# Batch 0's linear attention by token slot on 64x64 tiles, with the carried state added in PSUM, in a gated linear attention and channel mixer kernel on one Trainium2 core

## The chip, the cores and the metric

The kernel runs on one core of one Trainium2 chip. The metric is the device time of one execution in microseconds (us): three runs of the kernel before took 166.55, 166.55 and 166.72, median 166.55. The engines of a core are called as in the profile: PE (TensorE; PEld is its weight load), DVE (VectorE), ACT (ScalarE), POOL (GpSimd) and SP (SyncE, which here only issues transfers). Transfers are issued by SP and by ACT, each on a queue of its own.

## What is computed

Four batches, eight heads, 768 tokens, 48 channels per head. First a gated linear attention with a carried 48x48 state per head, then a mixer over tokens and one over channels, all on the 384 channels of the eight heads side by side:

```python
for t in range(S):
    state = alpha[:, :, t, :, None] * state + np.einsum('bhd,bhe->bhde', k[:, :, t], v[:, :, t])
    y[:, :, t] = np.einsum('bhd,bhde->bhe', q[:, :, t], state)
...
xt = x.transpose(0, 2, 1)
h = np.maximum(xt @ w_tok1, 0.0) @ w_tok2
u = x + h.transpose(0, 2, 1)
h2 = np.maximum(u @ w_ch1, 0.0) @ w_ch2
return (u + h2).astype(np.float32)
```

w_tok1 is 768x256, w_tok2 256x768, w_ch1 384x1536, w_ch2 1536x384; inputs and output are float32.

## The kernel before

**Chunks.** The attention is done in chunks of 256 tokens, three per batch, numbered n = 0 to 11 over all batches (batch 0 is n = 0, 1, 2). A chunk lies with two neighbouring tokens per partition: token 2p + s of the chunk is in partition p, in token slot s (0 or 1). Partitions 0 to 63 are its half 0 (128 tokens), 64 to 127 its half 1. Each chunk loads alpha, k, q and v, 384 KB each (`ld_at`, `ld_kt`, `ld_qt`, `ld_vt`; L534).

**Decay.** The recurrence is made parallel by cumulative products of alpha: logarithms on ACT (`ln`), cumulative sums by a matmul with a triangular matrix (`cumw` for batch 0, `cum` for the others), exponentials on ACT (`E`, `IE`, and `Et` for the decay of a whole half). k is multiplied by IE (`kk`, L642), q by E (`qq`). Batch 0 (`WIDE`) does this for both slots apart; the others first multiply the alphas of the two slots (`P`, L578) and adjust k and q (`k0a`, `q0r`).

**Within a chunk.** k and q are transposed on PE (`trk`, `trq`) and copied out of PSUM (`evk`, `evq`); from n = 6 on transfers do it (`dk`, `dq`, `pq`). `G` (gmm) makes the products of k and q for one half, 128x128 per head, as 16 matmuls on 64x64 tiles; `mask` (L700) copies them with a causal mask. `y` (ymm) multiplies them with v, contracting over the 128 tokens of a half in one matmul per head; `i` (inter) adds q times the state carried into that half; `x` copies the result as the mixer's input, 128 tokens by 384.

**The halves.** To contract over 128 tokens of one half, its two slots must fill 128 partitions, while they lie in 64 partitions side by side. So half tiles are copied to the other partitions: of v by `vs0`, `vs1` (vswap), of k by `ka`, `kb`, `kc` (kturn; `kc` overwrites k in place, after `trk`). `K` (kfull) then makes both halves' sums of k times v, four matmuls each. The state after a half is (K + state before) times the decay: `sa` adds (L750, DVE), `sm` multiplies (L753, DVE or POOL); `s` (L747) is the multiplication alone where there is no state before.

**Mixer.** Per batch: `t1` (L787, 12 matmuls in two groups), relu `ht`, `t2` (L792, six results, each reads both pieces of w_tok2), `u` = x + t2 (L796), `up` transposes u on PE (L803) and `ut` copies it, `c1` (L811: 12 chunks of 128 of the 1536 columns, two halves of the tokens each, three matmuls of 384), relu `rt`, `c2` (L816: four groups of three matmuls for each of six token blocks), `o` adds u (L820), `st` stores. From batch 2 on a transfer transposes u (`ux`).

**Weights.** They are loaded in pieces of 384 KB (`ldw_`) and cast to bf16 (`cw_`): wt1 and wt2 in two pieces each, wc1 in six (piece 3h + c is the half h of the columns, 128 of the 384 rows), wc2 in six.

**Order.** Nothing is scheduled when the kernel is built: `ORDER` lists every operation with its engine as the last letter (t PE, s ACT, v DVE, g POOL, y SP), and each engine runs its own in that order. `BUFS` gives the buffer of each tile in turn. Waits follow from the data and the buffers; an operation that overwrites a buffer waits for its readers. All raw loads share the buffers of class `in`, of which there are 19. An operation marked `port` (the copies and products that both DVE and POOL can do) also waits for the last marked one on the other of these two engines (`shared`). A transfer signals on one of eight semaphores, and waits for the transfer that last used its semaphore. Fillers (`f1_`, `f3_`) are matmuls of zeros, 512 wide, that keep PE busy before an operation.

## Time and profile before

| | us |
|---|---|
| median of three runs | 166.55 |
| span of the profiled execution | 165.0 |
| busy: PE, DVE, ACT, POOL | 156.2, 121.2, 96.2, 68.7 |
| busy in the first 30 us: PE, DVE, ACT, POOL | 24.4, 21.6, 23.1, 14.9 |
| matmuls of zeros (x38) | 12.7 |
| c1 and c2 matmuls (x588) | 106.0 |

The profiled execution's own time is the span and what lies around it; 1.55 us separate the span from the median of the runs. The granted clock reads full in every slice. PE waited longest for a first result of DVE (1.2 us in two waits), for the memset of the zeros (1.1) and for two copies on ACT (1.0 and 0.9).

Line numbers with L are those of the kernel before. Matmuls go through a helper, so L593 stands for many of them, and L684 and L685 for the copies on ACT and on DVE or POOL. Times in the timeline are the start in us from the start of the span, and the duration.

### The profile page before, as it was taken

The page shows a single profiled execution, that of the slowest core. Times are in us where ns is not written, and L with a number is a line of the kernel's source. Part 1 is how long each engine was busy: PE and PEld are TensorE (multiplying, and loading weights), DVE is VectorE, ACT ScalarE, POOL GpSimd, SP SyncE. Part 2 cuts the span into 40 slices and gives each one's busy share as a digit, 9 for nine tenths or more (in the row PEclk, how much of TensorE's full clock was granted, in tenths as well). Part 3 has the DMA queues.
Part 4 walks back from the last instruction along what each step waited for, and adds up shares of the span by engine and source line. Part 5 has one row for each costly group of instructions (what it writes and reads, how often), then busy time and mean ns, then how long its engine had stood idle before and what let it go on. Part 6 is the DMA issues. An engine that isn't in the chain of part 4 may idle for free.

```text
span 165.0 us, 4235 instructions
## 1 busy us (share of the span) xinstructions
PE 156.2 (95%) x1683; PEld 99.2 (60%) x1683; DVE 121.2 (73%) x210; ACT 96.2 (58%) x186; POOL 68.7 (42%) x84
## 2 busy tenths in 40 slices
PE   7969769999999999999999999999999999999992
PEld 2435446666666766576666666666666656656662
DVE  4098989989898898798878999989492455524422
ACT  3599987998877837939887746913614001514110
POOL 4025659497217475792388528973300000000000
PEclk9999999999999999999999999999999999999999
DMA  4999999999999999999989996898001136200213
GB/s 121 324 325 325 337 347 316 365 327 352 371 335 347 326 315 226 307 252 264 136 198 255 211 250 120 219 181 183 0 4 48 49 75 157 105 0 0 99 72 119
DMA packets 74531, 34.48 MB, mean 209 GB/s; under 512 B 67984, under 2 KB 73488, under 8 KB 74512
## 3 DMA queue, kind: packets, MB, share of 16 engines
q1 hardware_dynamic: 50576, 23.30, 55.2%
q10 hardware_dynamic: 23936, 10.91, 24.3%
q8 instruction: 13, 0.21, 0.5%
q14 instruction: 6, 0.05, 0.1%
HBM read 25.17 MB, written 4.72 MB: 181 GB/s over the span
## 4 chain that ended last, share of the span: by engine, by line
PE 83%; DMA 4%; SPq 3%; POOL 2%; issue 2%; ACT 2%; DVE 1%; POOLq 0%; DVEq 0%
PE ps L816 29%; PE ps L811 29%; PE ps L593 14%; PE ps L792 5%; DMA in<-in_v_dram 4%; PE ps L787 4%; SPq L534 3%; PE ps L654 1%; PE ps L803 1%; POOL pkk L642 1%; DVE gtm L700 1%; POOL vb L685 1%; ACT x L684 1%; POOL ss L753 1%; ACT E L626 0%
## 5 line engine op out<-in xcount | busy, mean ns | idle before, releaser
L816 PE MATMUL ps<-wc,rt 128*128 128x384 bf16 (+1 forms) x300 | 54.7, 320 | 0.0
L811 PE MATMUL ps<-ut,wc 128*128 128x384 bf16 x288 | 51.3, 326 | 0.0
L782 ACT ACTIVATE rt<-ps 128x384 bf16<-128x384 f32 x54 | 24.4, 490 | 35.4 <-PE ps L811 34.7
L811 PEld LDWEIGHTS <-wc 128*128 128x128 bf16 x288 | 27.1, 98 | 16.7
L816 PEld LDWEIGHTS <-rt 128*128 128x128 bf16 x300 | 27.5, 98 | 15.9
L700 DVE TENSOR_TENSOR gtm<-ps,mk 128x1024 bf16<-128x1024 f32 x24 | 28.7, 1219 | 4.8 <-PE ps L593 3.4
L784 DVE TENSOR_SCALAR rt<-ps 128x384 bf16<-128x384 f32 x42 | 21.7, 551 | 9.2 <-PE ps L811 9.2
L820 DVE TENSOR_TENSOR o<-ps,u 128x384 f32<-128x384 f32 (+1 forms) x25 | 13.1, 537 | 10.0 <-PE ps L816 9.1
L685 POOL CAST vb<-in 64x384 bf16<-64x384 f32 (+1 forms) x18 | 10.9, 608 | 15.2 <-DVE pkk L642 8.9
L593 PE MATMUL ps<-zs 128*128 128x512 bf16 x38 | 12.7, 452 | 2.9 <-DVE zs L496 1.1
L684 ACT CAST x<-ps 128x384 bf16<-128x384 f32 x17 | 7.8, 477 | 10.7 <-PE ps L593 10.5
L796 DVE TENSOR_TENSOR u<-ps,x 128x384 bf16<-128x384 f32 x24 | 11.8, 550 | 3.0 <-PE ps L792 3.0
L642 DVE TENSOR_TENSOR pkq<-in,E 128x768 bf16<-128x768 f32 x8 | 7.6, 954 | 5.4 <-ACT E L626 5.2
L787 PE MATMUL ps<-x,wt 128*128 128x384 bf16 x48 | 11.1, 325 | 0.5 <-DVE gtm L700 0.4
L684 ACT CAST vb<-in 64x384 bf16<-64x384 f32 (+1 forms) x18 | 11.1, 618 | 0.7 <-DMA in<-in_v_dram 0.2
L642 POOL TENSOR_TENSOR pkk<-in,IE 128x768 bf16<-128x768 f32 x5 | 9.1, 1816 | 4.9 <-DVE pkk L685 3.2
L753 POOL TENSOR_TENSOR ss<-tmp,E 128x384 bf16<-128x384 f32 x11 | 9.2, 833 | 3.2 <-DVE tmp L750 2.9
L750 DVE TENSOR_TENSOR tmp<-ps,ss 128x384 f32<-128x384 f32 x16 | 8.8, 552 | 1.0 <-PE ps L593 0.5
L792 PE MATMUL ps<-ht,wt 128*128 128x384 bf16 x48 | 9.5, 326 | 0.0
L593 PEld LDWEIGHTS <-gtm 128*128 128x128 bf16 x192 | 7.4, 96 | 2.7 <-DVE gtm L700 0.9
L593 PEld LDWEIGHTS <-tpk 48*64 48x64 bf16 x384 | 6.1, 106 | 4.9 <-issue 4.3
L593 PE MATMUL ps<-vb,gtm 128*128 128x48 bf16 x192 | 8.6, 183 | 0.4 <-DVE gtm L700 0.4
(91 smaller groups left out, 216.6 us busy)
## 6 DMA issues: line engine op xcount, KB each, us to landing
in<-in_moe_w_ch_dram SPq DMA_DIRECT2D x10, 384.0 KB, 6.2
in<-in_alpha_dram SPq DMA_DIRECT2D x9, 384.0 KB, 6.8
out_dram<-o SPq DMA_DIRECT2D x16, 192.0 KB, 2.5
in<-in_q_dram SPq DMA_DIRECT2D x7, 384.0 KB, 6.3
in<-in_v_dram ACTq DMA_DIRECT2D x7, 384.0 KB, 6.0
in<-in_k_dram ACTq DMA_DIRECT2D x6, 384.0 KB, 5.7
in<-in_k_dram SPq DMA_DIRECT2D x6, 384.0 KB, 6.2
in<-in_v_dram SPq DMA_DIRECT2D x5, 384.0 KB, 7.2
```

The source lines that it names most:

```text
L593: return self.pe.matmul(out, lhsT=lhsT, rhs=rhs, start=start, stop=stop, skip_group_check=True)
L642: self.shared(self.eng[e].tensor_tensor(self.t(dst)[:, :, :, 0:D], self.t(src).rearrange("p h s d -> p s h d"), bass.AP(tensor=f.tensor, o ...
L684: return self.act.copy(d, s)
L685: return self.shared(self.eng[e].tensor_copy(d, s))
L700: self.nc.vector.tensor_tensor(self.t(gtm)[:, hf, :, :], self.pair(gp).rearrange("p a (j t) -> p (a j) t", t=128), bass.AP(tensor=m.tensor ...
L782: self.act.activation(d, s, AF.Relu)
L784: self.nc.vector.tensor_scalar_max(d, s, 0.0)
L787: self.pe.matmul(self.bank(bank)[:, 0:HD], lhsT=self.wt1[:, kc, m * 128 : m * 128 + 128], rhs=self.t(x), start=(kc == 0), stop=(kc == NS - 1))
L792: self.pe.matmul(self.bank(bank)[:, 0:HD], lhsT=self.wt2[:, kc, i * 128 : i * 128 + 128], rhs=self.t(hts[kc]), start=(kc == 0), stop=(kc = ...
L811: self.pe.matmul(self.bank(bank)[:, 0:HD], lhsT=self.wc1[:, kc, mc * 128 : mc * 128 + 128], rhs=self.t(ut)[:, 3 * half : 3 * half + 3, kc, ...
L816: self.pe.matmul(self.bank(bank)[:, 0 : cz - ca], lhsT=self.t(rts[mc][0])[:, i * 128 : i * 128 + 128], rhs=self.wc2[:, mc, ca:cz], start=( ...
L820: self.nc.vector.tensor_tensor(self.t(o)[:, ca:cz], self.bank(bank)[:, 0 : cz - ca], self.t(u)[:, i % 3, ca:cz], ALU.add)
```

## The change

**Batch 0 by token slot.** For n = 0, 1, 2 the two slots stay where they lie. `gslot` computes for one slot of k (instead of one half) the products with q: output partitions 0 to 63 hold half 0's tokens of that slot, 64 to 127 half 1's. `maskslot` uses a mask for each slot (`mkw`, built by eight small copies at the start), still 128x1024 per instruction. `khalf` sums k times v on 64x64 tiles, per half, head pair and slot, 16 matmuls of 48 columns; `kadd` adds the state before in PSUM by one matmul with the identity; `s` then multiplies by the decay on DVE. `yslot` makes both halves of y in 32 matmuls that contract over 64 partitions. The copies `vs`, `ka`, `kb`, `kc` and the additions `sa` of batch 0 are gone. Chunks from n = 3 on do as before.

**Weight pieces.** Pieces 0 to 2 of wc1 are now 256 columns with all 384 rows each, so that chunks 0 to 5 of `c1` wait for one piece alone; pieces 3 to 5 are as before. The matmuls of zeros read a buffer of the relus instead of a tile of their own.

**Order.** `ORDER` and `BUFS` are new throughout: 954 operations are 923; of 22 fillers (38 matmuls) 5 are left (18 matmuls, eight of them before `cumw0`); of the 64 loads ACT issues 30, where it issued 24 (11 of the first 24, where it was 4 of the first 25); the loads use buffers 0 to 11 of class `in`, where they used all 19.

```diff
+        if wide:
+            for hf in range(nst):
+                kp, s_, sp = V("one"), V("ss"), states[-1]
+                KO = O(f"K{hf}_", {"PE": (160.0, 350.0)}, 9.5 + hf, writes=[kp], reads=[pkk, vb],
+                       preds=[kk, vc] + fill(f"K{hf}_", kp),
+                       emit=lambda e, hf=hf, kp=kp, sp=sp: g.khalf(kp, pkk, vb, hf, sp is not None), mode="G")
+                if sp is not None:
+                    KO = O(f"A{hf}_", pe([384]), 9.6 + hf, writes=[kp], reads=[sp[0]], preds=[KO, sp[1]],
+                           emit=lambda e, kp=kp, s0=sp[0]: g.kadd(kp, s0))
+                so = O(f"s{hf}_", dve(384), 10 + hf, writes=[s_], reads=[kp, E], preds=[KO, et],
+                       emit=lambda e, s_=s_, kp=kp, hf=hf, sp=sp: g.sfirst(s_, kp, E, hf, wide, sp is not None))
+                states.append((s_, so))
+        else:
...
+        if wide:
+            yo = O("y", {"PE": (640.0, 830.0)}, 14, writes=yps, reads=[gtm, vb], preds=masks + [vc] + helds[0] + helds[1],
+                   emit=lambda e, st=states[:2]: g.yslot(yps, gtm, vb, [not q for q in st]), mode="Y")
...
-                         reads=[ut], preds=(uts[0:2 + half] if b in UP else [uts[half]]) + [wl[("wc1", mc // 6 * 3 + p)] for p in range(3)],
+                         reads=[ut], preds=(uts[0:2 + half] if b in UP else [uts[half]]) + [wl[("wc1", p)] for p in ([mc // 2] if mc < 6 else (3, 4, 5))],
...
+        for h in (slice(0, 64), slice(64, 128)):
+            for sl in range(2):
+                w = self.mkw[h, sl].rearrange("p (t s) -> p s t", s=2)
+                dv.tensor_copy(w[:, 1], self.u2[h, h])
+                dv.tensor_copy(w[:, 0], (self.us if sl else self.u2)[h, h])
...
+    def gslot(self, gp, tpk, tpq, sl):
+        tk, tq = self.t(tpk), self.t(tpq)
+        for j in range(4):
+            for hf in range(2):
+                for r in range(2):
+                    pr = slice(r * 64, r * 64 + D)
+                    self.mm(self.bank(gp, r)[hf * 64 : hf * 64 + 64, j * 128 : j * 128 + 128],
+                            tk[pr, (sl * 4 + j) * 128 + hf * 64 : (sl * 4 + j) * 128 + hf * 64 + 64],
+                            tq[pr, j * 256 + hf * 128 : j * 256 + hf * 128 + 128], True, True)
...
+    def khalf(self, kp, pkk, vb, hf, spread):
+        kk, vv = self.t(pkk), self.t(vb)
+        ph, w = slice(hf * 64, hf * 64 + 64), 2 * D if spread else D
+        for j in range(4):
+            for sl in range(2):
+                for r in range(2):
+                    c = w * j + (D * r if spread else 0)
+                    self.mm(self.bank(kp)[r * 64 : r * 64 + 64, c : c + D], kk[ph, sl, 2 * j + r, :],
+                            vv[ph, sl, 2 * j + r, :], j == 0 and sl == 0, not spread and sl == 1)
+
+    def kadd(self, kp, s0):
+        self.mm(self.bank(kp)[:, 0:HD], self.idn, self.t(s0), False, True)
+
+    def yslot(self, yps, gtm, vb, first):
+        gg, vv = self.t(gtm), self.t(vb)
+        for h in range(H):
+            for sl in range(2):
+                for hf in range(2):
+                    ph = slice(hf * 64, hf * 64 + 64)
+                    self.mm(self.bank(yps[hf])[:, h * D : h * D + D], gg[ph, sl, 4 * (h % 2) + h // 2, :],
+                            vv[ph, sl, h, :], first[hf] and h == 0 and sl == 0, h == H - 1 and sl == 1)
```

The orders begin so (before, then after); a load is `ld_` or `ldw_` with its engine as the last letter:

```
ld_at1s ld_at0y ld_qt0y ld_vt0y ld_kt0s ld_at2y f1_cumw0t ln0s f3_cumw0t f1_trk1t f1_cumw1t f1_trk0t f3_cumw1t
f1_trq0t f3_trq0t ln1s ld_qt1y f1_trq1t cumw0t cumw1t E0s ld_at3y f3_trk1t IE0s Et0s qq0v vb0s ld_kt1y kk0v trq0t E1s
f3_cumw2t vs1_0g ld_vt1y evq0v trk0t ka0s vs0_0g f1_cumw2t evk0s ld_kt3y qq1v kb0s IE1s f1_G00t G0_0t P3g ld_qt2y
...
```

```
ld_at0s ln0s f8_cumw0t cumw0t ld_at1y ln1s ld_kt0y IE0s cumw1t Et1s kk0g f6_trk0t f1_trk0t trk0t E0s E1s ld_qt0y qq0v
f1_trq0t trq0t ld_at2y evk0v ld_vt0y vb0g ln2s cumw2t ld_kt1s Et0s K0_0t IE1s ld_qt1y kk1v qq1g evq0s E2s ld_qt2s qq2g
K1_0t G0_0t s0_0v Et2s ld_vt1y G1_0t trk1t mask1_0v IE2s ld_at3s evk1s f2_trq1t trq1t vb1s ib0t A1_0t ld_kt2y mask0_0v
P3v ld_kt3y ld_vt2y s1_0v y0t trq2t K0_1t x0_0v kk2v ld_vt3s evq1s G0_1t x1_0s lnP3s A0_1t s0_1v ldw_wt10s evq2s ln13s
ld_qt3s cum3t k0a3g IE3s G1_1t mask1_1v kk3g vb3g mask0_1v ldw_wt11s ldw_wt21s trk2t K1_1t A1_1t ldw_wt20y evk2s E3s
r13s G1_2t mask1_2v G0_2t ldw_wc14y vb2s kb3g ib1t ia1t y1t ld_at4s ka3s trk3t ldw_wc13y K0_2t s1_1v A0_2t cw_wt10s
t1_0_1_0t x0_1s t1_0_0_0t mask0_2v vs1_3s t1_0_0_1t ldw_wc15s t1_0_0_2t vs0_3g cw_wt11s ia2t kc3g K3t ld_kt4y s0_2v
ib2t y2t x1_1s ldw_wc12y t1_0_1_1t t1_0_1_2t q0r3g qq3g t1_0_0_3t x0_2s evk3v t1_0_1_3t t1_0_1_4t cw_wt20g s0_3v x1_2v
...
```

## The prediction

> **What bounds the kernel now.** I read the granted clock and the 40 slices first, then the chain of waits in order of time, the table of stretches, the landings of the loads, and the timeline of the first 37 us on each engine. In the slices (the page's second part) PE and DMA say most:
>
> ```profile
> PE   7969769999999999999999999999999999999992
> DVE  4098989989898898798878999989492455524422
> PEclk9999999999999999999999999999999999999999
> DMA  4999999999999999999989996898001136200213
> ```
>
> From the seventh slice on PE is busy 90% or more, to the end; the clock is granted in full; DMA is full for the first half, and DVE has little to spare until slice 29. The chain gives the seam exactly (start, duration, what):
>
> ```profile
> 9.15 1.15 SPq L534
> ...
> 10.34 1.15 SPq L534
> ...
> 14.06 7.23 DMA in<-in_v_dram
> ...
> 31.39 0.86 PE ps L787 x4
> ...
> 32.99 2.06 PE ps L792 x12
> ...
> 37.51 2.48 PE ps L811 x15
> ...
> 156.81 5.16 PE ps L816 x42
> 161.97 0.03 issue
> 162.02 0.04 issue
> 162.06 0.36 DVE o L820
> ```
>
> Up to 31.4 us loads and vector work set the pace: SP's queue lets one 384 KB load through every 1.15 to 1.26 us. From 31.39 to 162.0 the chain is PE without a gap over 0.04 us, then one result and its store, 3.0 us. So the end is the moment from which PE has no more gaps, plus the PE work then left. The change alters batch 0's attention, nearly all before that moment. I therefore compare the first channel-mixing matmul (L811), 37.51 in the row, and what PE has done by then. Token mixing's second matmuls (L792) start at 32.99.
>
> The landings, in us after the issue, from stretches at 9.2, 14.5 and 17.1 us:
>
> ```profile
> in<-in_k_dram SPq DMA_DIRECT2D x1, 384.0 KB, 4.8
> ...
> in<-in_k_dram ACTq DMA_DIRECT2D x1, 384.0 KB, 5.9
> ...
> in<-in_moe_w_tok_dram ACTq DMA_DIRECT2D x1, 384.0 KB, 5.7
> ```
>
> SP's load waits behind its own queue; ACT's two had nearly none of their own, and yet took longer. The trace's packets of that k load on ACT's queue run only from 17.26 to 19.81: 2.7 us after the issue, then 2.55 us beside SP's, against 1.21 for a load that runs alone. An ACT load costs 5.8 us while SP's queue is full; a second behind it comes 2.5 us later.
>
> **The change part by part.**
>
> **Vector work taken out.** Thirteen half copies (vs six, ka and kb two each, kc three; 0.50 on POOL, 0.51 on ACT, L684 and L685) make 6.6 us, four additions (L750, 0.56) 2.2 us; four multiplications stay, now on DVE from PSUM (L747, 0.55). 8.8 us over three engines is 2.9 us at the best, if nothing else ends last. Setup gains eight small mask copies on DVE; the same engine waits 5.2 us for the first exponential (before 8.52), which hides them (0.2 us each by L519's row, 1.6 us if bare).
>
> **PE.** K takes 80 matmuls where 20 were, y 96 where 48 were, 4 additions by the identity come in: 112 more net, of small size. No row shows them; the nearest is G's (L593, 64x64 tiles), 0.42 us for 16 alone, 0.285 in the chain: 2.0 to 2.9 us. PE's useful work in the first 30 us is some 24.4 (the stretches) less 12.7 of filler: 18 us of cover, so I take zero; at the end of a chain, y's 32 cost at most 0.4 more than before. Fillers go from 38 to 18.
>
> **The clock at the start.** The fillers' weight loads come 0.427 us apart until the row at 5.72, and 0.2 after: full speed came after 4.7 us of unbroken work. Now eight fillers end 3.4 us after the first, and PE stands until the first logarithm ends. That starts at 5.6 instead of 5.0, its load now being ACT's (landing rows 4.8 against 4.2), so the first cumulative sum starts at 6.5 (6.62 before). I take half speed for both sums: 1.7 us each for 0.88 (L593 rows at 6.62 to 7.50). Bounds: 0 and 1.6 us. The Trainium skill ("TensorE: Matmul & The Clock Gate", Part 1) says that a busy free-running window of about 3.4 us releases the clock; by it the sums would be slow here unless a window fell just on the fillers, the same 1.6 us; the 4.7 us of the rows above agree with a window that began after the first filler.
>
> **Loads.** Of the first 24 loads 11 are now ACT's (4 of 25 before), and they rotate over 12 buffers instead of 19, so more wait for a reader. Step by step, ACT's load at 5.3 us (between 4.8 and 5.8) where its queue is empty:
> - k of n=1 is issued behind ln2, after the second sum's Et1: 10.2, landing 15.5. Before: issued 9.15, landed 13.95, kk1 at 14.54. Now kk1 starts 15.6 and ends 16.5.
> - Behind kk1 on DVE stand s0_0 and both masks of n=0, to 19.4 (0.5 and twice 1.17). alpha of n=3 goes into kk1's buffer: issued 16.6, landing 21.9. P3, on POOL at 12.94 before, is now on DVE and waits for it, 2.5 us, with s1_0, x0_0, kk2 and three masks queued behind.
> - From P3 to x1_2 stand seven 384-wide operations (0.48 apart), kk2 (0.86), four masks (1.17), evk3 (0.65): 9.6. x1_2 runs 31.5 to 32.05. Before, the last x (ACT, L684) ended at 31.72.
> - wt10 is issued behind lnP3, 22.4, landing 28; on the same queue follow qt3, wt11, wt21 at 1.2 to 2.5 each: wt21 lands between 31.6 and 33 (27.5 before). Its cast (0.83) stands on ACT ahead of ht_0_0: 32.4 to 33.8. On POOL, each operation waiting for its marked neighbour on DVE, k0a3, kk3 (1.82), vb3, three halves, q0r3, qq3 (1.82) put the cast of wt20 at 32.05.
> So three chains meet at t2: last three t1 (0.5), drain 0.2, ht 0.55 after x1_2 give 33.4; wt21 33 to 34.3; wt20 32.1. I take 33.4, +0.4 on 32.99. From there to L811 the row of before needs 4.52, 0.27 of it a sum of n=5 that now comes later: 33.4 + 4.25 = 37.65. The third of the three pieces that c1's first chunk needs, wc15, is last but one on ACT's queue (behind at4): landing 36.4 to 37.4, cast 0.82: 37.2 to 38.2, no later in the middle. That the other half of wc1 comes in pieces that serve two chunks alone gives nothing here, as chunk 11 is first and needs three whole pieces. Its shorter runs (1024 B) cost nothing by wt1's row, 5.7.
>
> **Later stages.** From L811 on, work is the same; the 0.27 us sum is still to do. Counted on PE's order with these rows, three places now have 0.8 to 1.0 us of PE work between a c1 and the c2 that reads its relu (1.2 was the least), and the chain needs 0.2 + 0.5 + 0.07. DVE's share falls by about 10 us (work goes to POOL), so I charge 0.1 each: 0.3; bounds 0 and 1.5.
>
> Sum: 0.14 + 0.27 + 0.3 = +0.7 us on the profiled execution: span 165.0 becomes 165.7. The median of the runs is 1.55 above that span; with it 167.3.
>
> **The rivals.**
>
> *Loads land as with SP (4.8, no sharing).* Then kk1 starts 14.9, alpha lands 20.9, x1_2 ends 31.0, wt21 lands by 30.4; with a clock that is released a further 1.1 comes off. t2 at 31.3 to 32.3, L811 at 35.6 to 36.6, the removed 2.9 us showing in part: -1.9 to -0.9, less 0.27 and some of the 0.3 given back: 164.9 to 166.0. For it: before, SP's queue alone moved as many bytes. Against: the two ACT rows above, and 2.5 us of DVE standing for P3. 0.36.
>
> *The ACT queue starves channel mixing* (the other side). wt21 and wc15 take 2.5 us each because kt4, wc12, at5 and qt4 run on SP beside them. wt21 at 33, wc15 at 38.2 or a load later, 39.4, cast 0.8: L811 at 39 to 40, 1.5 to 2.5 later: 168.3 to 169.5. It decides from wc15 landing after 36.8. For it: DMA is full up to slice 18. Against: SP itself waits for casts in between. 0.15.
>
> *Later weights come late.* Twelve buffers let loads run less far ahead: wc22 and wc23 are issued by ACT at about 45 and 48 and land 5.8 later, and second mixing wants them at 53.7 and 57. Missing by one load costs 1.2, by two 2.4 us: 168.5 to 169.7. For it: DMA shows no free slice before the 20th. Against: the order asks for no load early that it does not need. 0.09.
>
> *64x64 does not pay.* If the four quarters do not overlap, each matmul still costs no more than the 0.02 to 0.026 us of G's rows; the 18 us of cover takes it. It gives the forecast's time.
>
> **How the numbers follow.** The forecast has 0.40, and by its own bounds (clock released, wt21 at 31.6 or at 33) 166.1 to 167.9. About 0.2% (0.33 us) is what a measurement here can tell from no change: 0.05 of the forecast's chance and 0.02 of the first rival's lie within it, 0.02 of the forecast's below. Faster: 0.34 + 0.02 = 0.36; same 0.07; slower: 0.33 + 0.15 + 0.09 = 0.57. The range takes the first rival's good end with 0.3 for a quicker alpha load, and the later-weights rival nearly whole: 164.6 to 169.8.
>
> **What would show it.** L792 starting near 33.4 and L811 near 37.6, with ACT's wt21 cast just ahead. P3 (L578) on DVE with an idle of 2 to 3 us put down to the alpha load. kk1 (L642, DVE) at 15 to 16. First sums with 0.32 us matmuls. PE full from L811 on, but for a few tenths. I am wrong if ACT's loads land in under 5 us, if L811 starts before 36.5, or if PE has over 1 us of gaps behind it.

## The result, and the profile after

The changed kernel takes 182.8 us (median of 4 runs, 181.0 to 183.4) against 166.55 us (166.46 to 166.72) for the kernel before: a ratio of 1.093, 95% interval 1.086 to 1.100. It is slower, as forecast, but by 16.3 us where 0.7 was forecast and 169.8 was the end of the range. The profiled execution has a span of 179.3 us (165.0 before). Executions more than 1.5% above the fastest of their kernel are left out of the ratios and times below (one of s6 took 863 us, which nothing here explains); the profiles of a9 and s5 are of such executions, and so these two have no start and rest.

The first view is again the 40 slices of the span, one digit for the busy tenths of each:

```profile
PE   7595679998899989999896999989889999999972
DVE  6035369777598966759787977979593551563412
PEclk9998765799999999999999999999999999999997
DMA  5999989997999976999999986796700133212042
```

Before, PE was at 9 from the seventh slice to the last but one. Now it is at 5 to 7 in four of the second to sixth slice, and behind them it falls to 8 in turns and once to 6. DMA, which was full from the second to the 20th slice, has holes from the sixth on. And the granted clock, which was full, is below that from the fourth to the eighth slice, with 5 in the seventh as the lowest.

Two numbers split the loss. The first matmul of channel mixing (L863, L811 before) starts at 41.67 instead of 37.34 us: 4.3 us are lost ahead of it. From there to the end of the span it takes 137.6 instead of 127.7 us: 10.0 us are lost behind it. (Second token mixing starts at 37.44 instead of 32.90.) I call these two the start and the rest below; the rest is the span less the start.

Ahead of the seam, DVE's timeline shows what was late first (start, duration, engine, line, operation; in brackets the idle time before it and what ended it):

```profile
16.95 2.36 DVE L740 TENSOR_TENSOR gtm<-ps,mkw 128x1024 bf16<-128x1024 f32 x2 [0.63 <-PE ps L617]
24.19 0.56 DVE L602 TENSOR_TENSOR in<-in 128x384 f32<-128x384 f32 x1 [4.88 <-DMA in<-in_alpha_dram]
24.66 0.55 DVE L799 TENSOR_TENSOR ss<-ps,E 128x384 bf16<-128x384 f32 x1
```

The product P3 waits 4.9 us for alpha of group 3. DVE has nothing else it may do, since s1_0, x0_0, kk2 and three masks stand behind it. That load was issued on ScalarE's queue at 15.88, and the landings of the stretch from 13 to 17 us give its time:

```profile
in<-in_moe_w_ch_dram SPq DMA_DIRECT2D x2, 384.0 KB, 7.1
...
in<-in_alpha_dram ACTq DMA_DIRECT2D x1, 384.0 KB, 8.2
```

The second row is that load: 8.2 us, and not 5.3 as I took it. What stands behind it is in ScalarE's timeline (ACT is its work, ACTq the loads that it issues):

```profile
21.16 0.48 ACT L708 CAST x<-ps 128x384 bf16<-128x384 f32 x1
24.78 0.52 ACT L608 ACTIVATE la<-in 128x384 bf16<-128x384 f32 x1 [3.14 <-DVE in L602]
24.86 0.38 ACTq L568 DMA_DIRECT2D in<-in_moe_w_tok_dram  x1
...
25.34 1.22 ACTq L552 DMA_DIRECT2D in<-in_q_dram  x1
...
26.71 0.49 ACTq L568 DMA_DIRECT2D in<-in_moe_w_tok_dram  x1
...
27.23 0.50 ACTq L570 DMA_DIRECT2D in<-in_moe_w_tok_dram  x1
```

These rows are one chain. lnP3 (L608) waits for P3, and P3 for alpha. The load of wt10 is *behind lnP3 in the same queue*, so it is issued at 24.86, and q of group 3, wt11 and wt21 follow it. A late load holds up work, and that work holds up the next loads: from 20 to 34 us the DMA engines move 283 GB/s, against 341 in the kernel before (mean of the stretches 20 to 26 and 26 to 34, by length).

Behind the seam there is no single place. The waits of PE from 41 us to the end (who waited for whom, sum in us, times, longest):

```profile
PE ps L863 <- ACT rt L834: 1.6, 1, 1.6
PE ps L868 <- DVE o L872: 1.4, 1, 1.4
PE ps L863 <- DMA ut<-u: 1.0, 1, 1.0
PE ps L617 <- DVE ss L805: 1.0, 1, 1.0
PE ps L617 <- DVE tmp L802: 0.9, 1, 0.9
PE ps L868 <- ACT wc L708: 0.6, 1, 0.6
PE ps L617 <- ACT rt L834: 0.5, 1, 0.5
PE ps L863 <- DVE rt L836: 0.5, 1, 0.5
```

The same view of the kernel before is empty: not one wait long enough to be listed. The eight waits make 7.5 of the 10.0 us; the other 2.5 are in no single row. The first line is at 45 us, and ScalarE's timeline gives its reason: two loads of the first channel weight take ScalarE's sequencer 1.99 us to issue, a third load 0.50, and behind them stand two logarithms and the relu that PE needs, which comes at 45.09.

```profile
41.53 1.99 ACTq L573 DMA_DIRECT2D in<-in_moe_w_ch_dram  x2
43.55 0.50 ACTq L552 DMA_DIRECT2D in<-in_v_dram  x1
...
45.09 0.47 ACT L834 ACTIVATE rt<-ps 128x384 bf16<-128x384 f32 x1
```

### The profile page after: what moved, and what is told of

Same layout as the page of the kernel before. It is cut to its first block, busy times and chain, and to the rows that moved or that the text cites. A ratio compares the mean times of both kernels' runs of the same rounds, so it can differ in the third digit from the quotient of the medians.

```text
span 179.3 us, 4412 instructions
## 1 busy us (share of the span) xinstructions
PE 160.5 (90%) x1775; PEld 102.8 (57%) x1775; DVE 113.7 (63%) x209; ACT 95.8 (53%) x179; POOL 76.3 (43%) x83
## 4 chain that ended last, share of the span: by engine, by line
PE 33%; DMA 13%; POOL 12%; DVE 8%; ACT 4%; issue 3%; ACTq 2%; DVEq 0%; POOLq 0%
PE ps L868 13%; PE ps L863 13%; DMA tpk<-pkq 5%; DMA out_dram<-o 4%; DMA in<-in_alpha_dram 4%; PE ps L617 3%; POOL pkq L666 3%; POOL pkk L666 3%; DVE o L872 2%; PE ps L839 2%; POOL in L602 2%; POOL tpq L709 1%; DVE u L848 1%; PE ps L844 1%; ACTq L552 1%
## 5 line engine op out<-in xcount | busy, mean ns | idle before, releaser
L863 PE MATMUL ps<-ut,wc 128*128 128x384 bf16 x288 | 53.9, 326 | 3.3 <-ACT rt L834 1.6
L834 ACT ACTIVATE rt<-ps 128x384 bf16<-128x384 f32 x53 | 24.2, 492 | 33.4 <-PE ps L863 33.3
L863 PEld LDWEIGHTS <-wc 128*128 128x128 bf16 x288 | 26.9, 97 | 21.0 <-issue 3.5
L724 DVE TENSOR_TENSOR gtm<-ps,mk 128x1024 bf16<-128x1024 f32 x18 | 21.6, 1218 | 1.7 <-PE ps L617 1.6
L666 POOL TENSOR_TENSOR pkk<-in,IE 128x768 bf16<-128x768 f32 x9 | 16.3, 1815 | 13.1 <-ACT IE L650 6.4
L666 POOL TENSOR_TENSOR pkq<-in,E 128x768 bf16<-128x768 f32 x7 | 12.7, 1812 | 14.2 <-DVE in L662 6.4
L617 PE MATMUL ps<-tpq,tpk 48*64 48x128 bf16 x384 | 9.6, 236 | 3.5 <-DVE ss L799 1.8
L658 POOL TENSOR_TENSOR in<-in,in 128x384 f32<-128x384 f32 x8 | 8.0, 1000 | 3.7 <-DVE pkk L666 3.6
L709 POOL CAST vb<-in 128x768 bf16<-128x768 f32 (+1 forms) x10 | 6.6, 662 | 6.5 <-DVE wc L709 5.2
L666 DVE TENSOR_TENSOR pkq<-in,E 128x768 bf16<-128x768 f32 x5 | 4.8, 955 | 7.2 <-POOL pkk L666 6.4
L617 PE MATMUL ps<-la,u 128*128 128x384 bf16 x18 | 6.0, 398 | 2.9 <-ACT la L611 1.9
L617 PEld LDWEIGHTS <-gtm 128*128 128x128 bf16 (+1 forms) x240 | 7.4, 98 | 2.0 <-issue 0.5
```

Source lines behind the costliest of these rows:

```text
L617: return self.pe.matmul(out, lhsT=lhsT, rhs=rhs, start=start, stop=stop, skip_group_check=True)
L666: self.shared(self.eng[e].tensor_tensor(self.t(dst)[:, :, :, 0:D], self.t(src).rearrange("p h s d -> p s h d"), bass.AP(tensor=f.tensor, o ...
L724: self.nc.vector.tensor_tensor(self.t(gtm)[:, hf, :, :], self.pair(gp).rearrange("p a (j t) -> p (a j) t", t=128), bass.AP(tensor=m.tensor ...
L834: self.act.activation(d, s, AF.Relu)
L863: self.pe.matmul(self.bank(bank)[:, 0:HD], lhsT=self.wc1[:, kc, mc * 128 : mc * 128 + 128], rhs=self.t(ut)[:, 3 * half : 3 * half + 3, kc, ...
```

## The experiments

I had four theories: the clock (the 20 fillers that are gone let it fall, and half speed costs the time); the loads on ScalarE's queue, or too few buffers for them; the new order of the later stages; and the 64x64 computation itself. Kernels named a start from the changed kernel, b from the kernel before, and s join the two orders. A letter at the end of an operation's name in the order is its engine (s ScalarE, y SP's queue, v VectorE, g GpSimd, t TensorE). All ratios are to the kernel before on the same chip. In the expectations of all but a1 to a4, starts of stages are counted from a zero 0.3 us earlier than in the profile's rows, so 37.64 there is 37.34 here; differences are the same.

| kernel | what it is | ratio, 95% interval | start | rest |
|---|---|---|---|---|
| before | | 1 | 37.34 | 127.7 |
| changed | | 1.093 (1.086 to 1.100) | 41.67 | 137.6 |
| a1 | changed, 25 more fillers | 1.071 (1.064 to 1.079) | 44.49 | 132.8 |
| a2 | changed, 19 buffers | 1.087 (1.078 to 1.095) | 42.48 | 136.3 |
| a3 | changed, all loads on SP | 1.040 (1.034 to 1.046) | 35.35 | 136.5 |
| a4 | new computation, old order | 1.018 (1.012 to 1.024) | 41.53 | 127.8 |
| a5 | a4, 12 more fillers | 1.024 (1.019 to 1.029) | 40.71 | 127.8 |
| b1 | before, 23 fillers fewer | 1.003 (0.999 to 1.008) | 38.52 | 127.6 |
| b2 | before, loads queued as in changed | 1.012 (1.008 to 1.015) | 38.69 | 128.4 |
| a6 | a3, 19 buffers | 1.042 (1.035 to 1.048) | 34.54 | 139.1 |
| a7 | a3, eleven products to DVE | 1.051 (1.044 to 1.058) | 35.51 | 137.3 |
| a8 | a3, smaller loads | 1.008 (1.005 to 1.011) | 33.44 | 133.1 |
| a9 | changed, smaller loads | 1.072 (1.067 to 1.076) | | |
| b4 | before, smaller loads | 0.998 (0.995 to 1.001) | 37.08 | 127.6 |
| s1 | a3 up to the seam, then old order | 1.017 (1.013 to 1.021) | 39.15 | 128.9 |
| s2 | s1, 15 more fillers | 1.037 (1.028 to 1.045) | 41.63 | 130.9 |
| s3 | s1, head of group 5 later | 1.038 (1.033 to 1.042) | 35.57 | 136.8 |
| s4 | s1, one load earlier | 1.005 (1.002 to 1.009) | 38.57 | 127.6 |
| s5 | s4, one product earlier | 1.005 (1.001 to 1.009) | | |
| s6 | s4, one sum later | 1.001 (0.998 to 1.005) | 36.01 | 129.7 |

### The clock

a1 puts fillers back where TensorE stood idle in batch 0:

```diff
-... f8_cumw0t cumw0t ... G1_0t ... trq2t ... A0_1t ...
+... f4_cumw0t f1_cumw0t f8_cumw0t cumw0t ... f8_trk1t G1_0t ... f8_trq2t f2_trq2t trq2t ... f2_G11t A0_1t ...
```

> The changed kernel with 25 fillers more (128x512 matmuls into PSUM that nobody reads), ahead of the first cumulative sum (5), of the second triangle of group 0 (8), of group 2's q transposes (10) and of the carried state of group 1 (2): in the trace of the changed kernel TensorE idles there for 1.9, 1.8, 2.4 and 0.4 us. Theory 1 (the lost fillers let the clock fall to half, 16.5 to 19.9 and 23.3 to 33.6 us, and that is the first 4.2 us of the loss): the granted clock stays at full there, token mixing's second step starts at 33.5 to 35 instead of 37.4, and the time falls by 2.5 to 4 us, to 179 to 180.5. Rival (loads and the engines that feed TensorE set these stages, and half speed only fills their waits): the clock rises, the second step still starts at 36.8 to 37.5, and the time stays within 1 us of 182.8.

Measured 179.1 us. The time fell by about what the clock theory said, and for another reason: the clock is at half for two slices still, and the second token step comes 2.4 us *later* than in the changed kernel (39.86 against 37.44), so nothing was gained ahead of the seam. The rest is 4.8 us shorter. Work that starts 2.8 us later loses 4.8 us less there. My reading is that it finds its loads landed by then; no run shows that by itself. So part of what the later stages wait for is not set by TensorE's own pace.

b1 takes the fillers away where the kernel before has them:

```diff
-... f3_trk1t ... f3_cumw2t f1_cumw2t ... f1_G00t G0_0t ... f3_trq1t trq1t ... f1_G10t ... f3_G02t f1_G02t ...
+... G0_0t ... trq1t ...
```

> The kernel before without its 23 fillers behind the two first cumulative sums (15 are left; the changed kernel has 18); everything else as it was. Theory 1 (TensorE's clock falls to half where batch 0's attention leaves it idle too much, and half speed there is on the path): a stretch of some us at half speed between 12 and 30 us, token mixing's second step 1.5 to 4 us after 33.2, and 168 to 171 us. Rival (half speed only fills waits for other engines): the granted clock falls but the second step stays within 0.7 us of 33.2 and the time within 1 us of 166.6.

The granted clock of b1:

```profile
PEclk9985556999999999999999999999999999999999
```

Five slices are below full speed, with the digits 8, 5, 5, 5 and 6. The second token step came 1.2 us later in the profile (34.07 against 32.90), and the measured ratio is 1.003, which does not differ from 1. The clock falls as the theory says and costs about 1 us at the start and next to nothing in the time; the 4.3 and 10.0 us are not of that size. a5 asks from the other side:

```diff
-... f1_G00t ... trq2t ...
+... f4_trq1t f1_G00t ... f8_trq2t trq2t ...
```

> The new computation under the old order (170.58 us, half speed at 21 to 27 us) with 12 fillers more, ahead of group 2's q transposes (8) and of the first triangle of group 0 (4). Theory 1: the clock stays at full and the time falls to 165.5 to 168; then the new computation costs nothing by itself. Rival (the 64x64 form makes TensorE wait for other engines): within 1 us of 170.6.

The clock is full in all 40 slices, the start is 0.8 us earlier than in a4, and the time is no shorter (1.024 against 1.018, the intervals meet). The clock theory falls as the main cause. Its price was measured in these two kernels; the changed kernel itself never ran with a full clock, since a1 did not lift it throughout.

### The queue of the loads

a2 changes only the buffer numbers of the loads, from 12 buffers in turn to 19:

```diff
-BUFS = """ 0 0 0 0 0 1 1 2 2 1 1 ...   (loads: 0 to 11)
+BUFS = """ ...                          (loads: 0 to 18, the one longest free)
```

> The changed kernel with the loads' tiles spread over all 19 buffers instead of 12; order and engines unchanged. Theory 2 (the loads come late because a buffer must first come free): the two casts and relus that TensorE waits for at 44.0 and 65.0 us in the changed kernel come in time, the ACT queue is not blocked at the issue of the second weight's loads (1.99 us at 41.5), and the time falls by 2 to 5 us, to 178 to 181. Rival (the loads are late because of the queue that issues them, or are not what TensorE waits for): 182 to 183.5, the gaps as before.

181.2 us: 1.6 us less, with intervals that overlap, and the start no earlier. ScalarE's timeline of a2:

```profile
14.24 0.55 ACTq L552 DMA_DIRECT2D in<-in_alpha_dram  x1
...
25.20 0.52 ACT L608 ACTIVATE la<-in 128x384 bf16<-128x384 f32 x1 [4.84 <-DVE in L602]
25.21 0.37 ACTq L568 DMA_DIRECT2D in<-in_moe_w_tok_dram  x1
```

Alpha of group 3 no longer waits for a buffer: it is issued at 14.24 instead of 15.88. It lands no sooner for that (from the landings of 12.5 to 17 us):

```profile
in<-in_alpha_dram ACTq DMA_DIRECT2D x1, 384.0 KB, 10.3
```

With 10.3 us it is there at 24.5 (24.1 in the changed kernel). wt10 is still issued behind lnP3, and lnP3 still waits 4.84 us for the product that needs alpha. The issue of the second weight's two loads, too, takes ScalarE as long as before (2.04 us at 42.41). Buffers are not what makes these late.

a3 moves the 30 loads to SP's queue, at the same places in the order:

```diff
-ld_at0s ... ld_kt1s ... ld_qt2s ... ld_at3s ... ld_vt3s ... ldw_wt10s ld_qt3s ... ldw_wt11s ldw_wt21s ...
+ld_at0y ... ld_kt1y ... ld_qt2y ... ld_at3y ... ld_vt3y ... ldw_wt10y ld_qt3y ... ldw_wt11y ldw_wt21y ...
```

> The changed kernel with all 30 loads that ScalarE issues moved to SP's queue, at the same places of the order. Theory 3 (ScalarE's queue is what is late: its loads take 8.2 us beside SP's, and where a load waits for its buffer everything behind it on ScalarE waits too): alpha of group 3 lands by 21 to 22 instead of 24.1, the waits on ScalarE's relu at 44.0 and on its casts at 65 go, and the time falls by 3 to 8 us, to 175 to 180. Rival (the loads are late as a whole, by their place in the order or by their buffers): the first tiles come later with a single queue, and the time is 182 to 186.

173.8 us, 9 us less than the changed kernel. SP's timeline of a3, the same loads:

```profile
12.68 0.37 SPq L552 DMA_DIRECT2D in<-in_alpha_dram  x1
...
18.72 1.43 SPq L568 DMA_DIRECT2D in<-in_moe_w_tok_dram  x1
```

Alpha of group 3 goes into the buffer that kk1 reads, so its issue follows kk1 on DVE, first in the changed kernel and then in a3:

```profile
14.89 0.96 DVE L666 TENSOR_TENSOR pkk<-in,IE 128x768 bf16<-128x768 f32 x1 [2.31 <-ACT E L654]
...
11.69 0.96 DVE L666 TENSOR_TENSOR pkk<-in,IE 128x768 bf16<-128x768 f32 x1 [1.05 <-DMA in<-in_k_dram]
```

kk1 runs 3.2 us earlier, as its k is issued at 6.78 on SP where it was issued at 9.89 on ScalarE. (The first row names ScalarE as what ended the wait, but that k lands 4.9 us after its issue, at 14.8, and kk1 follows it at once.) So alpha is issued at 12.68 instead of 15.88, and lands in 4.8 us instead of 8.2: 6.6 us earlier in all. P3 runs at 17.61 instead of 24.19, 6.58 us earlier, and channel mixing starts at 35.35 instead of 41.67, 6.32 us earlier. wt10 is issued at 18.72 instead of 24.86. The chain shown above accounts for the loss ahead of the seam, and more than it: without it the new batch 0 is 2 us ahead of the old. In the stretch from 15 to 25 us (start:end, length, then busy us of PE, PEld, DVE, ACT and POOL with instructions, clock, DMA share, GB/s), first of the changed kernel:

```profile
15.00:25.00 10.00, 6.06 (x110) 4.60 (x110) 4.49 (x6) 4.14 (x6) 3.62 (x2) 0.75 1.12 346
```

and then of a3:

```profile
15.00:25.00 10.00, 8.12 (x209) 6.20 (x207) 8.18 (x11) 8.35 (x14) 5.79 (x6) 0.80 1.07 300
```

All five engines do more, though the DMA engines move less. In this stretch it is which load comes when that counts, and not how many bytes are moved.

b2 asks whether that queue hurts in the old order too; it gives each load of the kernel before the queue that it has in the changed one:

```diff
-ld_at1s ld_at0y ... ld_at3y ... ld_kt1y ... ld_qt2y ... ldw_wt11y ldw_wt21y ... ld_qt3y ...
+ld_at1y ld_at0s ... ld_at3s ... ld_kt1s ... ld_qt2s ... ldw_wt11s ldw_wt21s ... ld_qt3s ...
```

> The kernel before with each load on the queue (SP's or ScalarE's) that the changed kernel gives it; order and buffers as before. 32 loads change their queue, 30 instead of 24 are then on ScalarE. Theory 3 (critical loads on ScalarE's queue beside a full SP queue land late, whatever the order and the computation): alpha and q of group 3 and the second token weight land 2 to 4 us later than before, token mixing's second step at 35 to 38, 169 to 173 us. Rival (ScalarE's queue hurts only in the new order): 166 to 168.

168.9 us, 1.2% slower, between the rival's range and the theory's, with the start 1.35 us later. So the queue costs there too, but a fraction. My reading is that it is dear where a load that others wait for stands behind work that itself waits for a load, which depends on the order; b2 shows only that the price differs.

### The computation and the order

a4 runs the new code under the old order:

```diff
-... vs1_0g ka0s vs0_0g kb0s kc0g K0t sa1_0v sm1_0g y0_0t y1_0t ...
+... K0_0t K1_0t A1_0t s1_0v y0t ...
```

> The code of the changed kernel (token slots, 64x64 tiles, no shifted copies in batch 0, state added in PSUM, the other pieces of the weight) under the order, engines and buffers of the kernel before, with the operations that are gone left out, the two y of a group joined at the later one's place and the state's products on VectorE. Theory 4 (the searched order is what costs the time, the new computation is worth about nothing): 164.5 to 168, the second step of token mixing at 32 to 33.5. Rival (the 64x64 computation itself costs the time, by its matmuls or by what it makes wait): over 172, with the loss ahead of token mixing. A third reading, a loss shared by both, lies between 168 and 172.

170.2 us, ratio 1.018, between the theories. The rest is 127.8, as before: the stages behind the seam lose nothing. The start is at 41.53, as late as in the changed kernel. The old order was laid out for other operations; that the new computation therefore does not fit it is likely, and I did not trace it. That leaves open what batch 0 is worth with an order of its own, for which s1 is made: the changed order, loads on SP, up to the first matmul of channel mixing, and from there the old order.

> The order of the changed kernel up to the first matmul of channel mixing (all loads in it on SP's queue), and from there the order of the kernel before. With all loads on SP the changed order reached channel mixing at 35.65 instead of 37.64 and lost 9.07 us in gaps afterwards; the kernel before took 124.6 us from there to TensorE's last matmul, and 4.3 us behind it and ahead of the count. Theory 4 (the later loss is the new order of the later stages alone): 35.65 + 124.6 + 4.3 = 164.6, range 164 to 166. Rival (what the new batch 0 leaves behind, loads less far ahead or other buffers, costs the later stages too): 168 to 173.

169.7 us, so the sum of 164.6 fell. One half of it nearly holds: the rest falls from 136.5 to 128.9 (127.7 before) with nothing but the later stages' part of the order changed, which holds their sequence and the queue of their loads together (the old order issues some of its loads from ScalarE). The other half does not: the second token step starts at 30.05, 2.85 us earlier than in the kernel before, and then the chain of s1 runs like this (start, duration, what):

```profile
30.41 6.16 DMA in<-in_alpha_dram
...
36.71 1.01 POOL in L603
...
37.74 0.44 ACT la L609
38.18 0.48 ACT E L645
...
38.70 0.60 PE ps L618 x6
39.30 2.79 PE ps L864 x9
```

The old order has the cumulative sum of group 5 ahead of channel mixing in TensorE's queue; its alpha was issued only at 30.41. That load, with the product and the sum behind it, is what holds channel mixing until 39.15.

### The rest

a6 gives a3 the 19 buffers (the buffer numbers of a2).

> The changed kernel with all loads on SP (173.84 us) and the loads' tiles over 19 buffers. Theory 2 (behind the start of channel mixing the new order loses 9.07 us because loads wait for buffers): the gaps behind 36 us fall to under 5 us, 168 to 171. Rival (they come from the order of the work on the other engines): 172.5 to 174.5, gaps of 8 to 9.5 us.

174.3 us, and the rest is no shorter (139.1). Too few buffers are not the cause here.

a7 moves the products from GpSimd to VectorE:

```diff
-k0a5g kk5g q0r5g P6g q0r7g kk8g q0r8g P9g P11g kk10g qq10g
+k0a5v kk5v q0r5v P6v q0r7v kk8v q0r8v P9v P11v kk10v qq10v
```

> The changed kernel with all loads on SP, and eleven products of the groups 5 to 11 (k and q by the exponentials, the products of alpha) on VectorE, where the kernel before has them, instead of GpSimd. Theory 5 (GpSimd, at 1.8 us for a product that VectorE does in 0.96, is what the later stages of the new order wait for): 169 to 172, gaps behind 36 us under 6 us. Rival (they are not what ends last): within 1 us of 173.8, or slower, since VectorE's own queue gets 8 to 10 us more.

175.5 us, slower than a3 by 1.0%. GpSimd's products are not what the rest waits for, or VectorE cannot take them.

a8, a9 and b4 make the loads themselves smaller: from batch 1 on, the loads of k, q and v bring four of the eight heads, and the others keep what the buffer held, so a part of the attention is computed from old data.

```diff
+        if b > 0 and nm != "at" and v.buf in self.seen:
+            d, src = d[:, 0:4], src[:, 0:4]
```

> The changed kernel with all loads on SP (173.84 us), where the loads of k, q and v of the groups 3 to 11 bring only four of the eight heads once a buffer has been filled (the other heads keep what was there); all else is done. Some 27 loads are half as large, 13 loads or 16 us of the DMA engines less. Theory 6 (behind the start of channel mixing the new order waits for loads that land later than it was made for): the 9.07 us of gaps fall to under 4 us, 166 to 170. Rival (the order of the work on the engines and the DMA transposes and stores make the gaps): 172.5 to 174.5, gaps of 7 to 9 us.

> The changed kernel itself (30 loads on ScalarE) with the same smaller loads. Theory 6: most of the loss is loads, 171 to 176. Rival: 179 to 183.

> The kernel before with the same smaller loads, as a control: TensorE has only 0.39 us of gaps behind 37.4 us there, so both theories expect 165 to 167; a larger fall would say that the loads bound the kernel before too.

b4 does not differ from the kernel before: its loads do not bound it. a8 takes 168.6 us, 5.2 less than a3; by the spans 1.9 us of it are ahead of the seam and 3.4 in the rest. a9 takes 179.2 us, 3.6 less than the changed kernel and in the rival's range, which fits that its loads are late because they are issued late. So late loads are at least some third of what the rest of a3 loses (3.4 of 8.8 us; the loads were made smaller, not taken away); in a8 it is still 5.4 us longer than in the kernel before. The waits of PE in a8 behind 35 us:

```profile
PE ps L873 <- DVE o L877: 2.0, 1, 2.0
PE ps L868 <- DMA ut<-u: 1.3, 1, 1.3
PE ps L622 <- DVE tmp L807: 0.9, 1, 0.9
PE ps L622 <- DMA in<-in_q_dram: 0.3, 1, 0.3
```

None of the first three lines, 4.2 us together, is a load: the last results wait at the very end for their buffer and its store, a transpose of u by the DMA engines is late, and so is a sum on VectorE. These are the lines of the changed kernel again (1.4, 1.0 and 0.9 there). They stay when the loads are smaller, and are gone where the old order of the same stages is used (the rest is 127.6 in s4), so they belong to the new order with the queue of its loads. Why the new order has them I did not test.

### Towards a version that is faster

s2 is s1 with fillers:

```diff
+f2_cumw0t ... f3_trk1t ... f1_trq2t ... f3_G01t ... f2_G11t ... f4_G12t
```

> The same with 15 fillers more in batch 0's attention, where TensorE idles there. Theory 1: no half speed from 17 to 26 us, channel mixing begins 1 to 2.5 us earlier, 162.5 to 164.5. Rival (other engines set batch 0's end): the clock rises and the time stays within 0.5 us of the run without these fillers.

173.2 us, slower than s1: the start is 2.5 us later, and the clock falls in other slices instead. s3 moves the head of group 5's attention behind eleven matmul groups:

```diff
-... P5g lnP5s cum5t IE5s c1_0_8_0t E5s ln15s ... c1_0_9_1t ...
+... c1_0_8_0t ... c1_0_9_1t P5g lnP5s cum5t IE5s E5s ln15s r15s ...
```

> The splice (new batch 0 with its loads on SP, then the old order) with the head of group 5's attention (its product, log, cumulative sum, exponentials) moved from before channel mixing to behind its eleventh matmul group: the splice reached token mixing's second step at 30.35, and then TensorE stood still for 4.43 us at 34.5 because that cumulative sum, first in its queue, needed alpha of group 5, which had landed only at 36.57. Theory (the new batch 0 gains some 2.5 us when its loads are on SP, and only this seam ate it): channel mixing from 34.5 to 35.5, 164.5 to 166.5, faster than the kernel before. Rival (the loads are late as a whole there, and another wait comes in its place): 168 to 170.

173.7 us. Channel mixing began at 35.57, as hoped, but P5 now stood behind a weight's cast on GpSimd that waited until 41.58 for its load. P5 ran at 44.32, and TensorE waited 5.15 us in the middle of channel mixing. s4 moves one load instead:

```diff
-... ldw_wc14y ld_at4y ldw_wc13y ldw_wc15y ld_kt4y ldw_wc12y ld_at5y ...
+... ld_at5y ldw_wc14y ld_at4y ldw_wc13y ldw_wc15y ld_kt4y ldw_wc12y ...
```

> The splice (169.71 us: new batch 0 with its loads on SP, then the old order) with one load moved: alpha of group 5 is issued ahead of three pieces of the first channel weight, k of group 4 and a fourth piece, instead of behind them, five places of SP's queue earlier. In the splice it landed at 36.57 and TensorE stood still for 4.43 us for the cumulative sum made of it. Theory 6 (in this stage the DMA engines are full, 1.2 us for a load of 393 KB, so that the place in the queue sets when a load lands): it lands 4 to 6 us earlier, the gap falls to under 1.5 us, and the time to 165.5 to 168. Rival (the gap goes to the weights that now land 1.2 us later, or the stages behind pay): 168 to 170.

Ratio 1.005. The load was in time, but P5 stood behind three casts on GpSimd and ran at 36.29. s5 puts it ahead of them:

```diff
-... cw_wc14g ... P4g ... cw_wc13g ... cw_wc15g ... P5g ...
+... P5g cw_wc14g ... P4g ... cw_wc13g ... cw_wc15g ...
```

> The splice with the earlier load (1.0053 of the kernel before), and on GpSimd the product of alpha of group 5 ahead of the casts of three weight pieces instead of behind them: there alpha had landed by 32.2, but the product ran at 36.29, and TensorE stood still for 2.62 us at 35.9 for the cumulative sum made of it. Theory 6 (the new batch 0 is worth 1.5 to 2.5 us to the kernel once this seam is free, since its second token step starts at 31.4 instead of 33.2): channel mixing from 36.0 to 36.8 instead of 38.87, ratio 0.985 to 0.996. Rival (the casts, now 1 us later, hold channel mixing up instead, or the stages behind pay): ratio 1.000 to 1.008.

1.005 again: P5 now ran early, and the same sum waited for ScalarE's queue, where its logarithm stands behind those of group 4. s6 takes the sum out of the way:

```diff
-... cum5t k0a4g IE5s c1_0_8_0t E5s ut_0_2v ln15s ... c1_0_10_1t ... rt_0_8_0s ...
+... k0a4g c1_0_8_0t ut_0_2v ... c1_0_10_1t cum5t ... rt_0_8_0s IE5s E5s ln15s r15s ...
```

> The splice with the earlier load (1.0053), and the cumulative sum of group 5 on TensorE behind the first five matmul groups of channel mixing instead of ahead of them, with its exponentials behind the first relu on ScalarE; GpSimd as in that splice. Its three forms so far began channel mixing at 39.45, 38.87 and 38.81, each time for that sum, with another engine's queue ahead of it. Theory 6 (the new batch 0 gains once this sum does not stand in front): channel mixing from 36.3 to 37.2, when the cast of the last of the three weight pieces (35.5 to 36.3) is done, against 37.64 in the kernel before; ratio 0.990 to 0.998. Rival (the stage is bound by the loads, which the DMA engines bring one each 1.2 us whatever the order, so that a later wait returns the gain): ratio 1.000 to 1.010.

Ratio 1.001 (0.998 to 1.005): no difference from the kernel before. Channel mixing starts at 36.01, 1.33 us earlier than before, and the rest is 2.0 us longer. The largest part of that is a wait of PE for a relu. The timeline of s6:

```profile
39.20 0.49 ACT L647 ACTIVATE IE<-ps 128x384 f32<-128x384 f32 x1
39.59 0.50 ACT L644 ACTIVATE E<-ps 128x400 f32<-128x400 f32 x1
39.97 0.52 ACT L605 ACTIVATE lf<-in 128x384 f32<-128x384 f32 x1
40.53 0.52 ACT L614 ACTIVATE lf<-lf 128x384 f32<-128x384 f32 x1
...
40.96 0.48 ACT L708 CAST x<-ps 128x384 bf16<-128x384 f32 x1
...
41.33 0.83 ACT L708 CAST wc<-in 128x768 bf16<-128x768 f32 x1
42.07 0.49 ACT L834 ACTIVATE rt<-ps 128x384 bf16<-128x384 f32 x1
...
42.61 1.62 PE L863 MATMUL ps<-ut,wc 128*128 128x384 bf16 x9 [1.23 <-ACT rt L834]
```

ScalarE works without a pause from 39.20 until the relu at 42.07. The first four of these operations are those of group 5 that s6 itself has put there, so the time won ahead of the seam is in part lost to them behind it. A load is issued from ScalarE at 41.14 and takes 1.38 us, but it stands behind the relu in the order and does not hold it up. To move those four further back was not tried. No version here beats the kernel before.

With s6 the loss is split in two steps: from the ratio 1.093, moving the loads to SP takes it to 1.040, and the old order of the later stages, with one load and one sum moved at the seam, to 1.001; that is 0.053 and 0.039 of the time before. The second step changes the sequence of the later stages and the queue of their loads together, and no run here parts the two. The new computation of batch 0 is in all of these.

## Why the prediction failed

It said slower, and the sign is all that held. By its steps:

- *Vector work taken out, PE's extra small matmuls*: charged with nothing. s6 runs them all at 1.001, so together with the new order of batch 0 they cost nothing that could be measured. They bring little either: s6 starts channel mixing 1.3 us earlier, and that is not theirs alone, since the order and the queue of batch 0's loads are other too.
- *The clock at the start*: as forecast in kind (the two first sums at half speed). The later fall, between 16 and 34 us, was not foreseen. In two kernels near this one, b1 and a5, a lower clock was worth 1.2 and 0.8 us of the start and nothing clear in the time.
- *Loads, the first term that was mis-sized.* kk1 at 14.89 (15.6 forecast; its k landed in 4.9 us) and the issue of alpha at 15.88 (16.6) were close. The step that failed is "alpha of n=3: issued 16.6, landing 21.9", ACT's load at 5.3 us "where its queue is empty". Its queue was not empty: q of group 2 was issued on it at 13.64. The packets of these two loads in the trace run one behind the other, q's for 3.5 us and then alpha's for 2.7 us, beside SP's. My own sentence on a second load that comes 2.5 us later would have given 7.8 us; 8.2 were measured. A buffer that was free sooner did not help: in a2 alpha was issued 1.64 us earlier on the same queue and landed no earlier. P3 waited 4.88 us instead of 2.5, and wt10, behind it, was issued at 24.86 instead of 22.4. Then the work from P3 to x1_2 took 11.3 us instead of 9.6. Together: token mixing's second step at 37.44 instead of 33.4, a term of +0.4 on 32.99 that measured +4.5. From there to channel mixing, 4.25 were forecast and 4.23 measured.
- *Later stages, the second and larger one*: 0.3 us, "bounds 0 and 1.5"; measured 10.0. I had counted the distance between a c1 and the c2 that reads its relu on TensorE's order, and nothing else. None of the eight waits shown is that of a c2 for its relu. They are waits for ScalarE behind its own load issues, for VectorE's short sums and a relu (2.4 us in three lines), for results and their stores, for a DMA transpose and for a weight's cast, each in a queue that I had not walked. The prediction's own sign of being wrong, over 1 us of PE gaps behind L811, came true. That DVE had less to do said nothing of them.
- *The rival "Loads land as with SP"*, at 0.36, was right in what it said of its own case: it put channel mixing at 35.6 to 36.6 with such loads, and a3, with all loads on SP, started at 35.35, just before that. It went wrong in the same step as the forecast, the later stages. *"The ACT queue starves channel mixing"* (0.15) named the right culprit, and its 39 to 40 was nearest to 41.67; it saw the queue late for weights, and missed that an issue stands behind waiting work. *"Later weights come late"* by few buffers is refuted in its cause by a2 and a6. That the forecast had the sign right is luck in part: its +0.4 at the seam and 0.3 behind it stand for 4.5 and 10.0 us with other causes.

The Trainium skill ("DMA: Bandwidth & Descriptors", Rules for kernel authors) says that spreading transfers over several issuing engines brings no bandwidth, since they interleave on the same 16 DMA engines, and saves issue time alone. The trace agrees on the interleaving: the packets of the two loads above took 3.5 and 2.7 us beside SP's, against the 1.21 us for a load alone that the prediction names. a3 goes further than that: here the second queue did not save time, it cost 0.053 of the time before.

## What to carry to other kernels

A load issued from an engine that computes was issued here only when everything ahead of it in that engine's queue had what it waits for (wt10 at 24.86, 0.08 us after lnP3 began, for which ScalarE had waited 3.14 us). So walk that queue before you say when the load is issued, and ask whether what stands ahead of it waits for a load itself. Time won at one place need not arrive at the end: s6 starts channel mixing 2.56 us earlier than s4, and its span is 0.5 us shorter (165.7 against 166.2). And a new order must be costed over its whole length: here 10 of the 16 us were lost in stages whose computation was not changed.

## What the runs showed of the hardware

- The clock fell to half without one long idle stretch. In b1 it is at 0.74 of full from 8 to 14 us and at 0.50 from 14 to 26, while PE was busy for 2.82 us of the first 6 and for 9.94 of the next 12; by the trace the fall is at 10.84 us. The longest idle stretch that had ended by then is 1.0 us; the longest near it, 1.9 us, had begun 0.3 us before the fall. The kernel before, with 4.76 us busy in the first of these stretches and 9.15 in the second, kept full speed. So several gaps close together were enough here. The Trainium skill ("TensorE: Matmul & The Clock Gate", Why this matters for your kernels) warns of idle gaps above some 3 us; by these rows shorter ones are enough.
- Issuing a load can hold the engine that issues it for over a microsecond (1.99 us for two on ScalarE at 41.53 in the changed kernel, 1.38 us for one in s6, against 0.38 us at 24.86). In the first of these a relu behind it came late, and TensorE waited 1.6 us for it.
- A load issued earlier on a second queue need not land earlier: in a2 alpha of group 3 was issued from ScalarE 1.64 us earlier than in the changed kernel, with q of group 2 ahead of it in both, took 10.3 us instead of 8.2, and landed 0.4 us later.
